# Attention before a routed expert layer: the global queries' scores and maxima go ahead of an even iteration's values, and GpSimd's half of the weight split behind the scalings

## Chip, cores and metric

The kernel runs on one core of a Trainium2 chip. The time is device microseconds of one execution of the whole program, from its first to its last instruction and what lies around them; the figure for a kernel is the median of its runs. Profiles come from one execution of their own.

## What is computed

Local and global attention feeds a mixture of experts with eight experts. Cut to what matters:

```python
# B, H, Sl, Sg, D = 8, 8, 512, 32, 64; window 32
k_all, v_all = concat([k_g, k_l]), concat([v_g, v_l])
out_g = softmax(scale * q_g @ k_all.T) @ v_all            # 32 global queries see all keys
s_l   = concat([scale * q_l @ k_g.T,                      # local queries see the global keys
                where(|i - j| <= 32, scale * q_l @ k_l.T, -1e9)])   # and a band of local ones
out_l = softmax(s_l) @ v_all
x     = concat([out_g, out_l])  as rows of 512            # 8 * 544 = 4352 rows
# rows with x @ w_skip > 0 go to the expert with the largest x @ w_gate:
out   = x + gate * (relu(x @ w1[e]) @ w2[e])              # other rows keep x
```

All of it is float32.

## The kernel before, in words

**Stages.** The first stage does the attention of all batches and, a few iterations behind, writes the rows, computes the logits of gate and skip, and sorts the rows into lists per expert. The second stage runs the experts one after the other. The change lies in the first stage, in a loop whose order is written out by hand for PE, DVE, ACT and POOL (`manual_schedule`, L700); each of these engines takes its instructions in exactly the order of the code. SP, which issues most DMAs, is ordered by the framework.

**Iterations.** One unit of work `u` is a pair of heads of one batch: 8 batches x 4 pairs = 32 units. Iteration `u` of the loop (L720) works on three units at once: `cur` (scores and exponentials), `prev` = u - 1 (normalization and transposes) and `old` = u - 2 (values). For a unit:

- `scores(hf)` (L336), called for hf = 0 and 1: eight matmuls write the scores of four query blocks into two PSUM banks (`pss`, L343). DVE then reads each bank twice, adding the mask and taking the row minimum of the negated scores (L355); ACT takes the exponential with its sum (L360).
- `normal` and `scale` (L383, L388): DVE sums and inverts (L385, L386); POOL multiplies half of the probabilities (L390). `normal(0)`, `scale(0)` run in the unit's own iteration, `normal(1)`, `scale(1)` at the beginning of the next.
- `turn(hf)` (L424): PE transposes four probability blocks into `pst` (L430), which DVE (hf = 0) or ACT (hf = 1) copies to `ptT` (L433). `turn_g` is DVE's own transpose of the part of the global keys (L458).
- `values`, `values_g` (L462, L487): PE multiplies with the values into two banks `pv` (L474, L481, L493); ACT copies the local queries' part out (L501); `gather_g` (L503): DVE sums the global queries' part (L508, L506).

**Global queries.** For every second unit (u even) the 32 global queries of two head pairs are scored together. `window_g` (L367) writes the scores of the global keys, 64 columns, into free columns of a bank of the *second* score block (columns 320 to 383 of `banks[1]`, L350), ahead of DVE's four reads of this block; `window_min` (L374) takes their minimum behind these reads. In u = 0 they have a bank of their own (`pwg`, L399). At the end of the even iteration, behind the transposes, `scores_g` (L395) issues: four matmul instructions against the 512 local keys into a third bank (`psg`, L405), DVE's minimum over them that carries on the window's (L409), and ACT's exponential over all 640 columns (L414). In the next, odd iteration `normal_g` (L418) inverts the sum and lets POOL scale (L422), behind `scale(1)`; at its end `turn_pg` (L438) transposes the result (L442, L443) for the values of this pair of units, and DVE and ACT copy it (L448, L451).

**PSUM.** Score blocks, `psg` and `psgT` share three banks with the tag `s`; rows, transposes and `psgL` share three with the tag `t`; the values have two (`v`).

**Expert weights.** From u = 4 to u = 19 each iteration ends by splitting half of a weight piece of 128 x 1024 in two parts (`split`, L175, called at L803): ACT casts it to the high part (L181) and POOL subtracts this to get the low part (L182). POOL's subtraction so stands in its queue ahead of the next iteration's `scale(1)`, the global scaling and `scale(0)`. The pieces are loaded by SP into two buffers (L159); a load into a buffer waits for the subtraction that read it last.

**Order of one iteration before**, as far as it matters: `scores(0)`; `normal(1)`, `scale(1)` of prev, and for odd u `normal_g`; the rows of an earlier batch; `values` and `values_g` of old; `turn_g(0)`; `normal(0)`, `scale(0)`, `scores(1)`; `gather_g`; `turn_g(1)`; `turn(0)`, `turn(1)` of prev; for odd u `turn_pg`; for even u `scores_g`; up to two of the sends of list entries on POOL; the weight load and split.

Of the kernel before, what the change touches and what calls it, by code (L numbers as in the profile page):

```python
# [10 lines left out]
F32 = mybir.dt.float32  # L11
# [17 lines left out]
QB = 64  # L29
# [14 lines left out]
def kernel(  # L44
# [25 lines left out]
    def ps_v(name):  # L70
        return ps.tile([P, 512], F32, tag="v", name=name, bufs=2)
# [70 lines left out]
    class Weights:  # L142
# [29 lines left out]
                        ),  # L172
                    )

        def split(self, eng, parts=1):  # L175
            if self.done < parts * self.n:
                i, k = divmod(self.done, parts)
                self.done += 1
                sl = slice(k * WC // parts, (k + 1) * WC // parts)
                hi, lo, raw = self.view(i, "h")[:, sl], self.view(i, "l")[:, sl], self.raw[i][:, sl]  # L180
                nc.scalar.copy(hi, raw)  # L181
                eng.tensor_sub(lo, raw, hi.bitcast(F32))  # L182

    weights = {0: Weights(0, wpool)}

    with ExitStack() as actx:
        stage = actx.enter_context(tc.tile_pool(name="stage", bufs=2))
# [132 lines left out]
        def pair(u):  # L320
# [12 lines left out]
            pg = pgs[u // 2]  # L333
            pgTs = {}

            def scores(hf):  # L336

                banks = [ps_s("pss") for _ in range(2)]
                for j in range(2):
                    for odd in range(2):  # L340
                        w = 4 * hf + 2 * j + odd
                        for h in range(2):
                            nc.tensor.matmul(  # L343
                                banks[odd][head(h ^ odd), j * W:(j + 1) * W],
                                q[head(h), w * QB:(w + 1) * QB], window(k[head(h)], w),
                                start=True, stop=True, skip_group_check=True,
                            )
                last = hf == 1 and u % 2 == 0 and u > 0
                if last:
                    window_g(banks[1][:, 2 * W:2 * W + QB])  # L350
                for odd in range(2):
                    for j in range(2):
                        i = 4 * hf + 2 * j + odd
                        m = m_first if i == 0 else m_last if i == NB - 1 else (m_even, m_odd)[odd]
                        nc.vector.tensor_tensor_reduce(  # L355
                            out=pt[:, i, :], in0=banks[odd][:, j * W:(j + 1) * W], in1=m,
                            scale=-0.125, scalar=3.0e38, op0=ALU.add, op1=ALU.min,
                            accum_out=nmx[:, i:i + 1],
                        )
                        nc.scalar.activation(  # L360
                            pt[:, i, :], pt[:, i, :], AF.Exp, bias=nmx[:, i:i + 1],
                            scale=-1.0, accum_out=sums[:, i, 0:1],
                        )
                if last:
                    window_min(banks[1][:, 2 * W:2 * W + QB])

            def window_g(dst):  # L367
                for w in range(2):
# [25 lines left out]

            def scores_g():  # L395

                sumg = sumgt[u // 2 % 2]
                if u == 0:
                    pwg = ps_v("pwg")  # L399
                    window_g(pwg[:, 0:QB])  # L400
                    window_min(pwg[:, 0:QB])
                psg = ps_s("psg")
                for w in range(2):
                    k4 = ks[(u + w) % NQ].rearrange("d r (f g) m -> d g r f m", f=2)
                    nc.tensor.matmul(  # L405
                        psg[w * QB:(w + 1) * QB, :], qgs[b % 2][:, p + w, :],
                        k4[:, 0:4, 0:4], start=True, stop=True,
                    )
                nc.vector.tensor_tensor_reduce(  # L409
                    out=sg[:, 0:512], in0=psg[:, 0:512], in1=m_glob,  # L410
                    scale=-0.125, scalar=nmg[:, 0:1], op0=ALU.add, op1=ALU.min,
                    accum_out=nmg[:, 1:2],
                )
                nc.scalar.activation(  # L414
                    pg, sg, AF.Exp, bias=nmg[:, 1:2], scale=-1.0, accum_out=sumg[:, 0:1],
                )

            def normal_g():  # L418
# [84 lines left out]
            def gather_g(odd):  # L503
# [7 lines left out]
                    )  # L511

            return SimpleNamespace(
                scores=scores, normal=normal, scale=scale, scores_g=scores_g,
                normal_g=normal_g, turn=turn, turn_pg=turn_pg, turn_g=turn_g,
                values=values, values_g=values_g, gather_g=gather_g,
            )
# [182 lines left out]
        with tc.manual_schedule(engines=engines):  # L700
            nc.vector.memset(ones, 1.0)
            load_pair(0)
            warm = ps_t("warm")
            for i in range(WARM):
                nc.tensor.matmul(
                    warm, ones, ones.unsqueeze(1).to_broadcast([P, 4, P]), start=True, stop=True
                )
            consts_early()
            for t in sumt + sumgt:
                nc.vector.memset(t, 1.0e-9)  # L710
            clear_batch(0)
            load_qg(0)
            load_pair(1)
            consts_masks()
            load_v(0)
            load_vg(0)
            load_v(1)
            make_identity(nc, ident)
            prev, old, first = None, None, slice(0, 1)
            for u in range(NU + 2):  # L720
                if u < NU and u % NP == 2 and u // NP + 1 < B:
                    load_qg(u // NP + 1)
                    load_vg(u // NP + 1)
                if u + 2 < NU:
                    load_pair(u + 2)
                if 2 <= u + 1 < NU:
                    load_v(u + 1)
                cur = pair(u) if u < NU else None

                def seam():  # L730
                    tick(1 if u < NU - 4 else 2)
                    if u >= NU - 2:
                        send_some(1)

                def late_rows():
                    for b, k in LATE_ROWS.get(u, ()):
                        batch_rows(b, k)
                    if u == NU - 1:
                        for k in range(5):
                            batch_rows(B - 1, k, (0,))  # L740

                if cur:
                    cur.scores(0)
                if u == 0:
                    consts_pool()
                if prev:
                    prev.normal(1)
                    prev.scale(1)
                    if u % 2 == 1:
                        prev.normal_g()  # L750
                bp, kp = divmod(u - 6, NP)
                if 0 <= bp < B - 3:
                    batch_rows(bp, kp)
                    if kp == 3 and bp % 4 == 3:
                        batch_rows(bp, 4)
                seam()
                if old:
                    old.values(0)
                    old.values(1)
                    old.values_g()  # L760
                if prev:
                    prev.turn_g(0)
                seam()
                if cur:
                    cur.normal(0)
                    cur.scale(0)
                    cur.scores(1)
                seam()
                if old:
                    old.gather_g(0)  # L770
                    old.gather_g(1)
                if prev:
                    prev.turn_g(1)
                late_rows()
                seam()
                if prev:
                    prev.turn(0)
                    prev.turn(1)
                seam()
                if u == NU:  # L780
                    index(first, 0)
                    gather(xfirst, six[:, 0, 0, :], (B - 1) * S)
                if prev and u % 2 == 1:
                    prev.turn_pg()
                if cur and u % 2 == 0:
                    cur.scores_g()
                seam()
                if u == 1:
                    clear_batch(1)
                    consts_late()  # L790
                send_some(2 if u < NU - 3 else 4)
                seam()
                prev, old = cur, prev
                if u == NU - 1:
                    tick(len(stages))
                    send_some(len(sends))
                    slots(first, 0)
                if u == 3:
                    weights[0].load()
                if u >= 4:  # L800
                    if u % 2 == 0:
                        weights[0].load()
                    weights[0].split(nc.gpsimd, 2)  # L803
            for k in range(5):
                batch_rows(B - 1, k, (1,))

# [277 lines left out]
```

## Time and profile before

| | |
|---|---|
| median of 3 runs | 502.52 us (501.07 to 505.88) |
| the profiled execution | 501.2 us |
| its span, first to last instruction | 499.4 us |
| busy PE / PEld / DVE / ACT / POOL | 454.5 / 367.2 / 300.0 / 290.8 / 228.2 us |
| granted TensorE clock, mean | 0.987 |
| HBM read and written | 82.91 and 14.67 MB |

Instructions are named by engine, line and the tiles they write and read: `PE pss L343` is a matmul of line 343 into `pss`. PE is the tensor engine, PEld its weight load (which overlaps it), DVE the vector engine, ACT the scalar engine, POOL GpSimd, SP the queue that issues DMAs. Views used:

- busy time by stretch: for each stretch of time (us from the span's start) the busy time of each engine with its instructions, the granted clock, the DMA engines' busy share and GB/s;
- waits: who waited for whom, total us, times, longest;
- timeline: start, duration, engine, line, operation, out<-in, shape; equal neighbours are merged (x16), and then the duration is that of all of them. In brackets: how long the engine had been idle before, and what ended that. Matmuls are pipelined: the next may start before the printed end, so the time that one costs PE is read from start to start.

Every fp32 matmul shows as two instructions on PE.

### The profile page before, as it was taken

The numbers are of one execution on the slowest core, as the hardware profiler recorded it, in microseconds if no ns is written. First come the engines' busy times: TensorE is split into PE (matmuls) and PEld (weight loads), VectorE is DVE, ScalarE is ACT, GpSimd is POOL, SyncE is SP. The second block draws the span as 40 slices with busy tenths as digits, with TensorE's granted clock in tenths as the row PEclk, the third lists the DMA queues.
The fourth block names the chain that finished last, engine by engine and source line by source line (L and its number), as shares of the span: only waits on it lengthen the run. The fifth ranks groups of instructions, "written<-read, shape, count | busy, mean of one in ns | idle before, by whom it ended". The sixth has DMA issues, their size and how long they took to land. (4 is left out here: it accounts for less than half of the span.)

```text
span 499.4 us, 13645 instructions
## 1 busy us (share of the span) xinstructions
PE 454.5 (91%) x4962; PEld 367.2 (74%) x4962; DVE 300.0 (60%) x1221; ACT 290.8 (58%) x883; POOL 228.2 (46%) x236
## 2 busy tenths in 40 slices
PE   8898999999989998888699999999999999999991
PEld 3575676676666776566597979798978989788881
DVE  6886767877657867784344318783923848157210
ACT  5688999899877888765342208481713635245200
POOL 6556666668864667767345015142300431023200
PEclk9999999999999999999799999999999999999997
DMA  8989888888977798720446406975740849203100
GB/s 250 274 294 319 255 278 243 286 281 188 282 207 229 241 190 265 162 65 2 150 170 170 158 24 197 366 235 191 249 153 7 278 174 323 82 26 129 46 15 17
DMA packets 50545, 93.32 MB, mean 187 GB/s; under 512 B 15596, under 2 KB 19948, under 8 KB 50448
## 3 DMA queue, kind: packets, MB, share of 16 engines
q1 hardware_dynamic: 44624, 81.83, 52.5%
q0 software_dynamic: 5824, 10.25, 6.2%
q8 instruction: 55, 0.90, 0.8%
q14 instruction: 42, 0.34, 0.2%
HBM read 82.91 MB, written 14.67 MB: 195 GB/s over the span
## 5 line engine op out<-in xcount | busy, mean ns | idle before, releaser
L360 ACT ACTIVATE prob<-prob,nmx 128x160 f32<-128x160 f32 x256 | 106.4, 418 | 16.4 <-DVE nmx L355 14.9
L390 POOL TENSOR_TENSOR prob<-prob,inv 128x640 f32<-128x640 f32 x64 | 80.1, 1257 | 32.1 <-ACT prob L360 15.4
L853 ACT ACTIVATE hh<-ph 128x256 fp32r<-128x256 f32 x72 | 27.7, 384 | 79.5 <-PE ph L848 74.1
L930 POOL DMA_INDIRECT out_dram<-yo,six x12 | 12.2, 1018 | 130.0 <-DVE yo L929 112.1
L864 PE MATMUL py<-w2h,hh 128*128 128x512 f32 x144 | 57.1, 397 | 0.0
L864 PE MATMUL py<-w2h,hlw 128*128 128x512 f32 x144 | 56.8, 395 | 0.0
L864 PE MATMUL py<-w2l,hh 128*128 128x512 f32 x144 | 56.7, 394 | 0.0
L343 PE MATMUL pss<-ks,qs 64*64 64x160 f32 x1024 | 50.9, 303 | 2.5 <-DVE nmx L355 1.6
L848 PE MATMUL ph<-xh,w1h 128*128 128x256 f32 x288 | 46.6, 284 | 3.7 <-ACT xh L834 1.5
L474 PEld LDWEIGHTS pv<-ptT,vw 128*64 128x64 f32 x1024 | 39.6, 137 | 12.1 <-issue 4.6
L360 ACT ACTIVATION_READ_ACCUMULATOR prob<-prob,nmx 128x1 f32 x256 | 48.3, 189 | 0.0
L343 PEld LDWEIGHTS pss<-ks,qs 64*64 64x64 f32 x1024 | 33.6, 132 | 19.7 <-issue 13.5
L854 DVE SCALAR_TENSOR_TENSOR hlw<-ph,hh 128x256 fp32r<-128x256 f32 x72 | 30.2, 420 | 29.4 <-ACT hh L853 24.1
L474 PE MATMUL pv<-ptT,vw 128*64 128x64 f32 (+1 forms) x1024 | 44.4, 237 | 2.9 <-issue 1.3
L848 PE MATMUL ph<-xh,w1l 128*128 128x256 f32 x288 | 45.5, 280 | 0.0
L848 PE MATMUL ph<-xl,w1h 128*128 128x256 f32 x288 | 45.4, 280 | 0.0
L848 PEld LDWEIGHTS ph<-xh,w1h 128*128 128x128 f32 x288 | 39.5, 192 | 6.6 <-issue 4.3
L430 PE MATMUL pst<-ident,prob 128*128 128x128 f32 x256 | 37.8, 282 | 6.2 <-POOL prob L390 5.0
L631 POOL DMA_INDIRECT lst<-dat,slu x34 | 34.3, 1008 | 19.1 <-DVE cni L949 10.6
L848 PEld LDWEIGHTS ph<-xh,w1l 128*128 128x128 f32 x288 | 39.2, 191 | 0.0
L848 PEld LDWEIGHTS ph<-xl,w1h 128*128 128x128 f32 x288 | 38.9, 190 | 0.0
L182 DVE TENSOR_TENSOR w1l<-raw,w1h 128x1024 fp32r<-128x1024 f32 x28 | 34.1, 1219 | 6.6 <-ACT w1h L181 5.0
(178 smaller groups left out, 939.7 us busy)
## 6 DMA issues: line engine op xcount, KB each, us to landing
raw<-in_w_dram SPq DMA_DIRECT2D x60, 512.0 KB
vw<-in_v_dram SPq DMA_DIRECT2D x32, 512.0 KB
ks<-in_kT_dram SPq DMA_DIRECT2D x32, 400.0 KB
out_dram<-xr SPq DMA_DIRECT2D x32, 256.0 KB
qs<-in_qT_dram SPq DMA_DIRECT2D x31, 256.0 KB
vgs<-in_vgl_dram SPq DMA_DIRECT2D x32, 64.0 KB
raw<-in_w_dram POOLq DMA_DIRECT2D x4, 512.0 KB
lst<-dat,slu POOLq DMA_INDIRECT x34
```

The lines of the kernel that those rows point to most:

```text
L182: eng.tensor_sub(lo, raw, hi.bitcast(F32))
L343: nc.tensor.matmul(banks[odd][head(h ^ odd), j * W:(j + 1) * W], q[head(h), w * QB:(w + 1) * QB], window(k[head(h)], w), start=True, stop= ...
L360: nc.scalar.activation(pt[:, i, :], pt[:, i, :], AF.Exp, bias=nmx[:, i:i + 1], scale=-1.0, accum_out=sums[:, i, 0:1],)
L390: nc.gpsimd.tensor_mul(pt[:, sl, :], pt[:, sl, :], inv[:, sl].unsqueeze(2).to_broadcast([P, 4, W]),)
L430: nc.tensor.transpose(pst[:, i * P:(i + 1) * P], pt[:, 4 * hf + i, 0:KW], ident)
L474: nc.tensor.matmul(pv[head(h), j * 96:j * 96 + n], vv[:, w, head(h)], ptT[:, w, h ^ odd, 0:n], start=j == 0, stop=False, skip_group_check= ...
L631: ins = nc.gpsimd.indirect_dma_start(out=lst, out_offset=bass.IndirectOffsetOnAxis(ap=slu[:, t:t + 1], axis=0), in_=dat[:, bs[j], t - 4 * ...
L848: nc.tensor.matmul(ph[:, 0:GRP], hl[a][:, c, f * P:(f + 1) * P], bb[:, c, :], start=i == 0, stop=i == 3 * NC - 1,)
L853: nc.scalar.activation(hh[:, f, :], ph[:, 0:GRP], AF.Relu)
L854: nc.vector.scalar_tensor_tensor(hlw[:, f, :], ph[:, 0:GRP], 0.0, hh[:, f, :].bitcast(F32), ALU.max, ALU.subtract,)
L864: nc.tensor.matmul(py, a[:, f, ts_], hl[bb][:, f, :], start=f == 0 and i == 0, stop=f == NF - 1 and i == 2,)
L930: ins = nc.gpsimd.indirect_dma_start(out=out, out_offset=bass.IndirectOffsetOnAxis(ap=sidx, axis=0), in_=yo, in_offset=None, bounds_check= ...
```

## The change

Three things move, and nothing else:

1. In an even iteration `window_g`, `window_min` and the matmuls and maxima of `scores_g` come between the rows of the earlier batch and the values of `old`. The window part now goes into free columns of `banks[1]` of the *first* score block, after the four DVE reads of that block have been issued; u = 0 is no exception any more.
2. The exponential of the global scores (now `exp_g`) stays where `scores_g` was.
3. `split` gets a list for POOL's subtraction; what is in it is issued in the next iteration behind `scale(0)` and `scores(1)`. ACT's cast stays.

```diff
-        def split(self, eng, parts=1):
+        def split(self, eng, parts=1, later=None):
...
                 nc.scalar.copy(hi, raw)
-                eng.tensor_sub(lo, raw, hi.bitcast(F32))
+
+                def rest():
+                    eng.tensor_sub(lo, raw, hi.bitcast(F32))
+
+                if later is None:
+                    rest()
+                else:
+                    later.append(rest)
...
+    subs = []
...
+            sides = {}
+
             def scores(hf):
...
-                last = hf == 1 and u % 2 == 0 and u > 0
+                last = hf == 0 and u % 2 == 0
                 if last:
-                    window_g(banks[1][:, 2 * W:2 * W + QB])
+                    side = banks[1][:, 2 * W:2 * W + QB]
...
                 if last:
-                    window_min(banks[1][:, 2 * W:2 * W + QB])
+                    sides[0] = side
...
             def scores_g():
-                sumg = sumgt[u // 2 % 2]
-                if u == 0:
-                    pwg = ps_v("pwg")
-                    window_g(pwg[:, 0:QB])
-                    window_min(pwg[:, 0:QB])
+                window_g(sides[0])
+                window_min(sides[0])
                 psg = ps_s("psg")
...
+
+            def exp_g():
                 nc.scalar.activation(
-                    pg, sg, AF.Exp, bias=nmg[:, 1:2], scale=-1.0, accum_out=sumg[:, 0:1],
+                    pg, sg, AF.Exp, bias=nmg[:, 1:2], scale=-1.0,
+                    accum_out=sumgt[u // 2 % 2][:, 0:1],
                 )
...
                 seam()
+                if cur and u % 2 == 0:
+                    cur.scores_g()
                 if old:
                     old.values(0)
                     old.values(1)
...
                     cur.scores(1)
+                while subs:
+                    subs.pop()()
                 seam()
...
                 if cur and u % 2 == 0:
-                    cur.scores_g()
+                    cur.exp_g()
...
-                    weights[0].split(nc.gpsimd, 2)
+                    weights[0].split(nc.gpsimd, 2, subs)
```

More of the change, by code (lines that the diff above doesn't have):

```diff
@@ L513, in pair @@
             return SimpleNamespace(
-                scores=scores, normal=normal, scale=scale, scores_g=scores_g,
+                scores=scores, normal=normal, scale=scale, scores_g=scores_g, exp_g=exp_g,
                 normal_g=normal_g, turn=turn, turn_pg=turn_pg, turn_g=turn_g,
```

## The prediction

> **What bounds the kernel now.** The page shows attention up to about 240 us, then the expert layers, which the change does not touch; they would only move. I read the busy time by stretch first. Iterations come in pairs: u even (with the scores of the global queries) and u odd. The bounds of the rows below are starts of a first score block: u = 4 to 20 (eight pairs), then u = 11 (odd), u = 12 (even), and u = 20 to the end of u = 31.
>
> ```profile
> 28.45:137.35 108.90, 100.11 (x1693) 73.00 (x1692) 81.15 (x480) 97.93 (x366) 75.56 (x69) 1.00 0.90 274
> 75.57:82.54 6.97, 5.81 (x104) 4.51 (x102) 5.10 (x31) 6.36 (x24) 4.45 (x4) 1.00 0.92 276
> 82.54:88.63 6.09, 6.09 (x105) 4.38 (x105) 4.56 (x29) 5.64 (x23) 4.15 (x4) 1.00 0.69 209
> 137.35:228.00 90.65, 81.33 (x1328) 60.37 (x1327) 66.05 (x394) 71.75 (x271) 61.13 (x65) 1.00 0.67 187
> ```
>
> The columns are PE, PEld, DVE, ACT, POOL, clock, DMA share, GB/s. The even iteration is all PE (6.09 of 6.09 us); one in two has a logits matmul more and takes 7.09 (68.48 to 75.57, rows below). The odd one is 6.97 us for 5.81 us of PE: something else sets it. The waits by engine, from 10 to 236 us, say what (total, times, longest):
>
> ```profile
> PE psgT L442 <- POOL probg L422: 5.6, 10, 0.6
> PE pst L430 <- POOL prob L390: 5.0, 10, 1.2
> ```
> ```profile
> ACT probg L414 <- DVE nmg L409: 9.9, 13, 1.7
> ACT xT L501 <- PE pv L493: 7.1, 8, 2.2
> ACT ptT L448 <- DVE ptT L448: 2.4, 10, 0.4
> ```
>
> PE waits for GpSimd's scalings, 10.6 us in all, and ACT waits 9.9 us for the maxima of the global scores. The timeline of u = 10 and 11 shows the chain behind it, PE first, then POOL, then ACT:
>
> ```profile
> 72.62 0.72 PE L343 MATMUL pss<-ks,qs 64*64 64x160 f32 x16
> 73.27 0.34 PE L369 MATMUL pss<-ks,qgs 128*64 128x64 f32 x4
> 73.54 1.09 PE L430 MATMUL pst<-ident,prob 128*128 128x128 f32 x8
> 74.56 1.08 PE L405 MATMUL psg<-ks,qgs 128*64 128x512 f32 x4
> 75.57 0.77 PE L343 MATMUL pss<-ks,qs 64*64 64x160 f32 x16
> 76.27 0.66 PE L540 MATMUL pr<-ident,xT 128*128 128x128 f32 x4
> 76.86 1.35 PE L474 MATMUL pv<-ptT,vw 128*64 128x96 f32 x32
> ...
> 78.22 0.67 PE L493 MATMUL pv<-pgT,vgs 64*64 64x128 f32 x16
> 78.71 0.72 PE L343 MATMUL pss<-ks,qs 64*64 64x160 f32 x16
> 79.37 0.66 PE L430 MATMUL pst<-ident,prob 128*128 128x128 f32 x4
> 80.63 0.66 PE L430 MATMUL pst<-ident,prob 128*128 128x128 f32 x4 [0.60 <-POOL prob L390]
> 81.84 0.66 PE L442 MATMUL psgT<-ident,probg 128*128 128x128 f32 x4 [0.55 <-POOL probg L422]
> ```
> ```profile
> 78.09 1.27 POOL L182 TENSOR_TENSOR w1l<-raw,w1h 128x512 fp32r<-128x512 f32 x1 [4.48 <-ACT w1h L181]
> 79.32 1.25 POOL L390 TENSOR_TENSOR prob<-prob,inv 128x640 f32<-128x640 f32 x1
> 80.53 1.25 POOL L422 TENSOR_TENSOR probg<-probg,ing 128x640 f32<-128x640 f32 x1
> ```
> ```profile
> 75.41 0.56 ACT L433 COPY ptT<-pst 128x512 f32<-128x512 f32 x1
> 76.58 0.83 ACT L414 ACTIVATE probg<-smg,nmg 128x640 f32<-128x640 f32 x1 [0.61 <-DVE nmg L409]
> ```
>
> Global scores on PE (74.56), their maxima on DVE, the global exponential on ACT (76.58), the weight cast behind it, the subtraction on POOL (78.09), the two scalings (79.32, 80.53), PE (81.84): one chain through five engines. It ends 6.97 us after 75.57 whatever PE has to do.
>
> **The change, part by part.** No instruction is added or removed except that u = 0 no longer has a bank of its own for its four window matmuls. *The subtraction goes behind the scalings.* It takes 79.32 - 78.09 = 1.23 us off POOL's part of the chain and waits for no cast any more; its own new place, after the first-half scaling, has room, for POOL is busy 4.45 of 6.97 us. *The exponential stays, its maxima come earlier.* ACT's 0.61 us wait goes. Both together: in the odd iteration the scalings start when the maxima and sums of its own first block are through, and I get 6.1 us for it (work of PE 75.57 to 79.37, 1.02 for eight transposes, 0.70 for the five of the global part: 5.52, with about 0.6 of waits left), 0.85 less.
>
> *The price is at the new place.* The window part (L369) now goes into the second bank of the first score block, after the four DVE reads of that block have been put in the queue; before, it went into the bank ahead of the reads. The waits above show that this program holds two accesses of one PSUM bank apart even if both read, and read different columns: ACT's copy L448 waited for DVE's copy L448 of the same bank 10 times, 2.4 us. So I take it that the window matmuls wait until the last of the four reads has ended, and with them all that PE has behind them: the global scores, the values, the second score block, the transposes. That no row shows: bounds are nothing (a write beside a read of other columns) and the full wait. I take the full wait, as it is nearest to the L448 row.
>
> The Trainium skill, "PSUM — Partial Sum Buffer", section "PSUM bank collisions raise a hardware error", has the rule for this: guard PSUM "by bank × quadrant (by bank is the simple version), not by address", for writes against reads as well. The L448 row agrees for two reads; no run here shows a write behind a read. By the rule the sum is the one below, without it the first rival's.
>
> Where do the reads stand? Rows of DVE, in order of time, from u = 10 and u = 11:
>
> ```profile
> 68.48 0.42 DVE L448 COPY ptT<-psgT 128x256 f32<-128x256 f32 x1 [0.22 <-PE psgT L442]
> 68.82 0.28 DVE L451 COPY ptT<-psgL 128x128 f32<-128x128 f32 x1
> 69.29 0.33 DVE L355 CUSTOM_DVE_ANT_0 prob<-pss,m_first 128x160 f32<-128x160 f32 x1 [0.19 <-PE pss L343]
> ...
> 70.03 0.32 DVE L355 CUSTOM_DVE_ANT_0 prob<-pss,m_odd 128x160 f32<-128x160 f32 x1
> ```
> ```profile
> 75.23 0.65 DVE L433 COPY ptT<-pst 128x512 f32<-128x512 f32 x1
> 75.80 0.73 DVE L409 CUSTOM_DVE_ANT_0 smg<-psg,m_glob,nmg 128x512 f32<-128x512 f32 x1
> ...
> 79.70 0.16 DVE L385 TENSOR_REDUCE inv<-sumt 128x4 f32<-128x8 f32 x1 [1.45 <-ACT prob L360]
> ...
> 81.67 0.65 DVE L433 COPY ptT<-pst 128x512 f32<-128x512 f32 x1
> ```
>
> The fourth read ends at 70.35, 1.87 us after the block began; PE is through with the rows of the batch after 1.29 (75.57 to 76.86), with a logits matmul after 2.29. So even as DVE stands now, 0.6 us are lost in every second even iteration. But DVE will be later, for a ring closes that was open. PE's second score block of the even iteration sends DVE and ACT on; ACT's exponential, cast and four exponentials of the odd iteration hold DVE's sums (79.70 waits 1.45 us for ACT today); behind these stand DVE's reads, copies and then the four reads that PE now waits for. Today PE does not wait for those. The ring, once round for a pair:
>
> - PE second score block (even) to ACT's copy: 75.41 - 72.62 = 2.79, and the copy, 0.5.
> - ACT: global exponential, cast and four exponentials to DVE's sums, 79.70 - 76.58 = 3.12.
> - DVE: sums, four reads, sums of the global rows, transpose, 81.67 - 79.70 = 1.97; copy L433, 75.80 - 75.23 = 0.57.
> - DVE: copies L448 and L451, 0.34 and 0.28; four reads, 70.35 - 69.29 = 1.06.
> - PE: window part 73.54 - 73.27 = 0.27, global scores 75.57 - 74.56 = 1.01, values 78.22 - 76.86 = 1.36, their global part 0.49, and the second block again.
>
> The sum is 13.76, with a handover to PE 13.8 us. A pair takes 108.90 / 8 = 13.61 today (6.09 + 6.97 = 13.06 without the logits, 14.06 with). In the ring the logits matmul (1.0 us) hides in the stall, the rest of it does not: of an even iteration of 13.8 - 6.1 = 7.7 us, 6.09 is work and 1.6 stall. So u = 4 to 19: 8 x 13.8 - 108.90 = **+1.5 us**. Bounds: -6.8 (8 x 0.85, no stall) and +4 (14.1 each, since route steps on DVE come into the ring).
>
> *Outside.* From u = 20 the pairs take 90.65 / 6 = 15.1 us and there is no cast: the ring (13.3) is not full, but the stall itself remains. From u = 26 PE has no rows of earlier batches at this place, so it would be ready 0.70 us after the block began (75.57 to 76.27), and the fourth read is much later, for u = 30:
>
> ```profile
> 213.23 0.77 PE L343 MATMUL pss<-ks,qs 64*64 64x160 f32 x16
> 216.21 0.32 DVE L355 CUSTOM_DVE_ANT_0 prob<-pss,m_odd 128x160 f32<-128x160 f32 x1
> ```
>
> It ends 3.3 us after, so 2.6 us of stall; at least 1.87 - 0.70 = 1.2 in u = 26 and 28, 0.6 in 20 and 24: 6.2 us, less some 2 that PE's waits for POOL give back there: **+4** (0 to +7). At the start, u = 0 now needs the second pair's keys right behind the first score block, and u = 2 has the constants of DVE ahead of the four reads: **+2** (0 to +3), an estimate by the same kind of stall.
>
> *SP.* The weight load waits for the subtraction that frees its buffer, and this comes some 5 us later in the iteration; keys and values are queued behind it on SP. I cost this at nothing, as PE nowhere waits for them in the views above; the third rival is the case that it isn't.
>
> **Sum.** +1.5 + 4 + 2 = +7.5 on the profiled execution's 501.2 us (span 499.4): 508.7. That execution lay 1.3 us under the median of the runs shown, 502.5 (501.07 to 505.88), so I predict **510 us**.
>
> **Rivals.** *First: the window matmuls don't wait for the reads* (other side). Place: L369 at the head of the global scores. For it: the columns are free of each other; against: the L448 row. The even iterations keep 6.09 and 7.09 and the odd ones take 6.1: 8 x 0.85 = 6.8 off, less about 2 where the global scores wait for the bank that ACT's copy L448 still reads, and some 1 off outside: 501.2 - 5.8 + 1.3, about 497. It decides as soon as the wait at L369 is under 0.8 us a pair. Chance 0.15.
>
> *Second: the stall is there, but the ring doesn't fill,* because DVE gets to the four reads as it does now, 1.87 us in. Then an even iteration without logits loses 0.6, one with them nothing, and every odd one gains 0.85: 4 x 0.25 + 4 x 0.85 = 4.4 gained in the middle, some 4 lost outside: 502. For it: DVE today is ready only 0.2 us before PE needs it (the 0.22 and 0.19 in the rows of 68.48 and 69.29), so little tells on which side it falls; against: with the odd iteration shorter, the same DVE and ACT work ends later in it. Chance 0.22.
>
> *Third: the keys come late,* because SP stands at the weight load. One us lost in each of the six even iterations with such a load on top: 516. Against: DMA engines are busy 0.90, not 1. Chance 0.05.
>
> **How the numbers follow.** The forecast has 0.58. Within the bounds of its own terms it runs from 503 to 516. The first rival lies at 497, the second at 502; taking all but half of the first and the top of the third gives 498 to 516. A measurement of this kernel tells about 1%, 5 us, from no change. Faster than 497.5: half of the first rival, 0.08. Slower than 507.5: three quarters and more of the forecast and the third, about 0.57. The rest, 0.35, is within 1%.
>
> **What would show it.** In the changed kernel's timeline the window matmuls (L369) of an even iteration without logits start some 1.5 us after the batch's transposes, released by DVE's read of the scores, and the wait list has PE waiting for this read as its largest wait. ACT's wait for the global maxima is gone, PE's waits for POOL fall from 10.6 us to under 5, odd iterations take about 6.1 and even ones 7.7 us. If L369 starts within 0.2 us of the transposes, the step on the bank is wrong; if it waits but starts about 1.9 us into the iteration, the ring is; if PE waits for a DMA there, the third rival is right.

## The result and the profile after

The changed kernel takes 518.94 us (median of 4 runs, 516.88 to 520.08) beside 504.2 us of the kernel before (4 runs, 501.07 to 508.99): ratio 1.029, 95% interval 1.025 to 1.033, so it is slower. A second series of it gave 519.8 us, 1.030 (1.022 to 1.038). The forecast was 510 us with a range of 498 to 516: the sign was right, the size was not. Line numbers of the changed kernel are higher by about ten: the score matmul L343 is L353, DVE's read of it L355 is L365, the window matmul L369 is L379, the global scores L405 are L412, ACT's copy L433 is L443, the transposes of the rows L540 are L550.

The profiled execution took 516.88 us, its span 515.2 us. Busy time by stretch, with the same starts of score blocks as bounds: u = 4 to 20, u = 11, u = 12, and u = 20 to the start of u = 31 (columns as in the first view of the prediction):

```profile
31.80:142.25 110.45, 97.79 (x1694) 73.47 (x1693) 79.07 (x479) 96.60 (x364) 74.63 (x68) 1.00 0.80 249
79.59:85.65 6.06, 5.65 (x102) 4.54 (x102) 4.30 (x30) 6.06 (x24) 3.84 (x4) 1.00 0.90 289
85.65:92.98 7.33, 6.04 (x106) 4.50 (x105) 5.27 (x30) 5.85 (x24) 4.80 (x5) 1.00 0.75 272
142.25:231.50 89.25, 74.01 (x1232) 55.51 (x1231) 59.91 (x360) 65.95 (x248) 57.80 (x62) 1.00 0.68 196
```

The stretch before the first bound is 31.80 us, 3.35 more than before. The middle is 110.45 us, 1.55 more, with odd iterations of 6.06 us (6.1 forecast) and even ones without logits of 7.33 (7.7 forecast). The end (the kernel before has its u = 31 at 219.99) is longer by 11.51 - 3.35 - 1.55 = 6.6 us. PE's largest waits, from 10 to 236 us:

```profile
PE pss L379 <- DVE nmx L365: 12.2, 9, 3.3
PE pr L550 <- ACT ptT L443: 4.9, 8, 0.9
...
PE psgT L452 <- POOL probg L432: 1.4, 5, 0.6
...
PE pst L440 <- POOL prob L400: 0.7, 1, 0.7
```

The first row is the announced wait: the window matmuls for DVE's reads of the scores. The last two are the waits for POOL, 10.6 us before and 2.1 now; ACT's wait for the global maxima is gone. The second row was not announced: the rows of an earlier batch wait for ACT's copy of the transposes. Both stand in u = 12; DVE, ACT and PE in order of time:

```profile
86.81 0.58 ACT L443 COPY ptT<-pst 128x512 f32<-128x512 f32 x1
...
87.44 0.66 PE L550 MATMUL pr<-ident,xT 128*128 128x128 f32 x4 [0.92 <-ACT ptT L443]
...
88.09 0.32 DVE L365 CUSTOM_DVE_ANT_0 prob<-pss,m_odd 128x160 f32<-128x160 f32 x1
...
88.47 0.34 PE L379 MATMUL pss<-ks,qgs 128*64 128x64 f32 x4 [0.38 <-DVE nmx L365]
```

The fourth read begins at 88.09 and is through at 88.41; the window matmuls start at 88.47, right behind it. So the wait is where it was put, but only 0.38 us of this iteration's stall is at L379, and 0.92 us stands ahead of it at L550. The window matmuls start 0.38 us behind the rows, not the forecast 1.5, and 2.82 us into the iteration; of the other signs set for this place (within 0.2 us, or about 1.9 us into the iteration) neither came out. In the middle's iterations with logits (u = 6, 10, 14 and 18) PE does not wait at L379 at all.

The next table has all profiles that follow, in us; "rest" runs from the start of u = 31 to the end of the span.

| kernel | start of u = 4 | u = 4 to 20 | u = 20 to 31 | rest | median | ratio to before (95%) |
|---|---|---|---|---|---|---|
| before | 28.45 | 108.90 | 82.64 | 279.4 | 503.9 to 504.9 | |
| before, second profile | 28.13 | 108.93 | 82.96 | 280.7 | | |
| changed | 31.80 | 110.45 | 89.25 | 283.7 | 518.94 | 1.029 (1.025 to 1.033) |
| changed, second profile | 32.59 | 110.50 | 87.75 | 289.5 | 519.8 | 1.030 (1.022 to 1.038) |
| order alone | 32.77 | 115.72 | 85.02 | 287.1 | 523.59 | 1.037 (1.030 to 1.044) |
| late subtraction alone | 28.36 | 105.25 | 81.29 | 284.4 | 500.12 | 0.988 (0.982 to 0.994) |
| window ahead of the reads | 27.96 | 106.63 | 83.00 | 284.8 | 505.84 | 1.002 (0.998 to 1.006) |
| window in the first bank | 31.26 | 108.06 | 83.42 | 283.2 | 509.25 | 1.009 (1.005 to 1.012) |
| window in a bank of its own | 28.40 | 107.45 | 83.97 | 285.4 | 505.34 | 1.000 (0.996 to 1.004) |
| new order in u = 4 to 19 only | 29.37 | 109.87 | 81.32 | 282.4 | 506.5 | 1.007 (1.003 to 1.011) |
| changed, cast in the odd iteration | 32.58 | 109.27 | 86.88 | 285.5 | 518.32 | 1.029 (1.019 to 1.039) |
| late subtraction, cast in the odd iteration | 28.11 | 104.17 | 81.20 | 284.6 | 498.59 | 0.989 (0.983 to 0.995) |
| late subtraction, global scores ahead of the transposes | 28.20 | 105.24 | 83.55 | 279.4 | 498.86 | 0.991 (0.986 to 0.995) |
| the same, cast in the odd iteration | 29.25 | 103.11 | 83.06 | 280.0 | 498.1 | 0.985 (0.978 to 0.993) |

### The profile page after: what moved, and what is told of

It is laid out like the page before. It is cut to its first block, busy times and chain, and to the rows that moved or that the text cites. A ratio compares the mean times of both kernels' runs of the same rounds, so it can differ in the third digit from the quotient of the medians.

```text
span 515.2 us, 13635 instructions
## 1 busy us (share of the span) xinstructions
PE 452.2 (88%) x4962; PEld 369.3 (72%) x4962; DVE 297.2 (58%) x1221; ACT 289.5 (56%) x883; POOL 227.9 (44%) x236
## 5 line engine op out<-in xcount | busy, mean ns | idle before, releaser
L944 POOL DMA_INDIRECT out_dram<-yo,six x12 | 12.2, 1018 | 136.3 <-DVE yo L943 118.4
L484 PEld LDWEIGHTS pv<-ptT,vw 128*64 128x64 f32 x1024 | 40.8, 138 | 17.4 <-issue 8.9
L353 PE MATMUL pss<-ks,qs 64*64 64x160 f32 x1024 | 50.5, 303 | 1.3 <-DVE nmx L365 0.7
L484 PE MATMUL pv<-ptT,vw 128*64 128x64 f32 (+1 forms) x1024 | 42.9, 237 | 4.6 <-ACT prob L370 1.6
L353 PEld LDWEIGHTS pss<-ks,qs 64*64 64x64 f32 x1024 | 33.7, 133 | 9.4 <-issue 3.2
L365 DVE CUSTOM_DVE_ANT_0 prob<-pss,m_even 128x160 f32<-128x160 f32 x96 | 28.1, 317 | 18.8 <-PE pss L353 18.7
```

What stands on the lines that cost most here:

```text
L353: nc.tensor.matmul(banks[odd][head(h ^ odd), j * W:(j + 1) * W], q[head(h), w * QB:(w + 1) * QB], window(k[head(h)], w), start=True, stop= ...
L365: nc.vector.tensor_tensor_reduce(out=pt[:, i, :], in0=banks[odd][:, j * W:(j + 1) * W], in1=m, scale=-0.125, scalar=3.0e38, op0=ALU.add, o ...
L484: nc.tensor.matmul(pv[head(h), j * 96:j * 96 + n], vv[:, w, head(h)], ptT[:, w, h ^ odd, 0:n], start=j == 0, stop=False, skip_group_check= ...
L944: ins = nc.gpsimd.indirect_dma_start(out=out, out_offset=bass.IndirectOffsetOnAxis(ap=sidx, axis=0), in_=yo, in_offset=None, bounds_check= ...
```

## The experiments

The theory: a write into a bank waits for every read of that bank, PE stands at the window matmuls for DVE's fourth read, and in the middle this closes a ring through ACT, DVE and PE. Rivals: the late subtraction costs the time (A); PE would wait for DVE there whatever the bank (B, E); the middle carries the loss (C); the pairs are not set by ACT (D).

### The two parts apart

The order alone leaves the subtraction where it was; the late subtraction alone is the kernel before with a list behind the second score block.

```diff
-                    weights[0].split(nc.gpsimd, 2, subs)
+                    weights[0].split(nc.gpsimd, 2)
```

> The order of the global scores alone, with the subtraction left where it was before the change. Theory (PE waits at the window matmuls for DVE's fourth read of the same bank, and a ring of 13.8 us per pair closes): the waits at L379 stay as they are, the odd iterations lose part of their gain because POOL's subtraction of 1.23 us is back in their chain; 519 to 523 us, where the changed kernel has 518.9. Rival A (the late subtraction, and the weight load that waits for it on SP, cost the time): back to 502 to 506.

```diff
                     cur.scores(1)
+                while subs:
+                    subs.pop()()
...
-                    weights[0].split(nc.gpsimd, 2)
+                    weights[0].split(nc.gpsimd, 2, subs)
```

> The late subtraction alone, on the kernel before. Theory: no wait is added, PE's waits for POOL (10.6 us before) fall by up to 1.23 us in each of the odd iterations 5 to 19; 496 to 501 us, where before has 504.2. Rival A (the late subtraction costs the time): 513 or more.

Measured: 523.59 us for the order alone, 500.12 us for the subtraction alone. The first is 0.6 us above the expected: its middle takes 115.72 us, its odd iterations 7.53, more than the 6.97 of before, and PE's waits for POOL are back at 10.1 us. Rival A is out: the late subtraction, with its late weight load on SP, is a gain of 1.2% (0.6 to 1.8%). The first of the next rows is its middle, 3.65 us shorter than before; the others are ACT's wait for the global maxima and PE's waits:

```profile
28.36:133.61 105.25, 98.35 (x1694) 72.94 (x1693) 79.50 (x480) 96.63 (x364) 74.51 (x68) 1.00 0.90 282
```
```profile
ACT probg L422 <- DVE nmg L417: 11.6, 15, 1.7
```
```profile
PE pr L548 <- ACT ptT L441: 4.5, 7, 0.9
PE psgT L450 <- POOL probg L430: 2.6, 5, 0.6
...
PE pst L438 <- POOL prob L398: 1.6, 3, 0.7
```

Two things are to be seen. ACT still waits for the maxima (11.6 us), and yet the odd iterations from u = 5 to 13 are down from 6.97 to 5.60 or 5.80 us: the late subtraction alone does that. The even ones are longer for it, 7.08 us for 6.09 in u = 8 and 7.83 for 7.09 in u = 6, so a pair gains 3.65 / 8 = 0.46 us in the mean. And PE's wait for ACT's copy, 4.5 us (0.4 before), is here without any wait at the window matmuls; that it comes with the shorter odd iteration, as ACT is no faster, is my reading.

### The window part ahead of the reads, in the other bank, and in a bank of its own

```diff
                 if last:
                     side = banks[1][:, 2 * W:2 * W + QB]
+                    window_g(side)
...
-                    sides[0] = side
+                    window_min(side)
...
-                window_g(sides[0])
-                window_min(sides[0])
```

> The changed kernel with the window matmuls in the same bank, but issued ahead of DVE's four reads (and the minimum behind them). Nothing writes the bank behind a read any more. Theory: the wait of PE at the window matmuls is gone in the middle, at u = 2 and from u = 26 on; pairs of about 13.1 us in the middle, 497 to 504 us in all (504 if the 4.3 us that the changed kernel lost inside the seventh expert stay). Rival B (the wait is not the bank's: DVE is late for PE at this place anyhow, and the wait only moves to the next matmul that needs DVE): 513 to 519.

```diff
-                    side = banks[1][:, 2 * W:2 * W + QB]
+                    side = banks[0][:, 2 * W:2 * W + QB]
```

> The changed kernel with the window part in the first of the two banks of the block (DVE reads that bank first, so its last read ends two reads, 0.65 us, sooner). Theory (dependency by bank, not by address): PE waits for the second read, not the fourth; 0.65 us less at u = 2 and in each of the six even iterations from u = 20, and 0.3 to 0.65 less in the eight of the middle, where the ring falls to 13.15 us and PE's own work takes over: 510 to 513 us. Rival B, or a wait on the whole block or on DVE's position: within 2 us of the changed kernel's 518.9.

```diff
...
             def scores_g():
-                window_g(sides[0])
-                window_min(sides[0])
+                pwg = ps_t("pwg")
+                window_g(pwg[:, 0:QB])
+                window_min(pwg[:, 0:QB])
```

> The changed kernel, every instruction in the same order on every engine, but the window part in a PSUM bank of its own from the three of the rows and transposes. Theory (PE waits at L379 for reads of the same bank, and for nothing else of DVE): no wait of PE for DVE's score reads is left at the window matmuls, 504 to 509 us (505.8 was had with the window part ahead of the reads; up to 3 us more where the three banks are short). Rival E (the place in the order costs the time, whatever the bank): 515 or more. If the seventh run of expert matmuls takes 25.8 us or more, as in the four profiles with the window part behind the fourth read, it goes by PE's order of instructions; if 24.0 to 24.4, by something that the waits bring.

Measured: 505.84, 509.25 and 505.34 us, where the changed kernel has 518.94 and 519.8. The second edit changes nothing but the bank, and takes 9.7 us off. Here is u = 30 of the changed kernel and then of this one, the last reads and the window matmuls:

```profile
224.84 0.32 DVE L365 CUSTOM_DVE_ANT_0 prob<-pss,m_odd 128x160 f32<-128x160 f32 x1
225.09 0.08 DVE L365 DVE_READ_ACCUMULATOR2_ANT nmx<- 128x1 f32 x1
```
```profile
225.22 0.34 PE L379 MATMUL pss<-ks,qgs 128*64 128x64 f32 x4 [2.69 <-DVE nmx L365]
```
```profile
217.66 0.32 DVE L365 CUSTOM_DVE_ANT_0 prob<-pss,m_even 128x160 f32<-128x160 f32 x1
217.91 0.08 DVE L365 DVE_READ_ACCUMULATOR2_ANT nmx<- 128x1 f32 x1
217.91 0.32 DVE L365 CUSTOM_DVE_ANT_0 prob<-pss,m_odd 128x160 f32<-128x160 f32 x1
218.15 0.08 DVE L365 DVE_READ_ACCUMULATOR2_ANT nmx<- 128x1 f32 x1
218.15 0.32 DVE L365 CUSTOM_DVE_ANT_0 prob<-pss,m_odd 128x160 f32<-128x160 f32 x1
```
```profile
218.04 0.34 PE L379 MATMUL pss<-ks,qgs 128*64 128x64 f32 x4 [0.93 <-DVE nmx L365]
```

With the window part in the second bank PE starts 0.05 us after the fourth read; with it in the first bank it starts 0.05 us after the second read (217.91 + 0.08), while the third and fourth are still to end. The columns are free of each other in both. So the program holds PE by the bank. The trace agrees here with the rule of the Trainium skill that the prediction named ("PSUM — Partial Sum Buffer", section "PSUM bank collisions raise a hardware error"), to guard by bank and not by address. With a bank of its own, nothing of DVE's reads of the scores is left in PE's waits at the window matmuls, though every engine has the same order; these are PE's largest waits there, and its wait for the logits' transposes:

```profile
PE pr L544 <- ACT ptT L437: 4.8, 7, 0.9
PE pr L527 <- ACT xr L545: 1.8, 1, 1.8
...
PE pq L563 <- ACT ptT L437: 1.5, 4, 0.4
```

Rivals B and E are out. The theory's own number was too good for the first edit, though: 505.84 us, not 497 to 504. Its middle is 106.63 us, 13.3 per pair and not 13.1; the odd iterations from u = 5 to 13 keep 6.06 to 6.4 us where the late subtraction alone has 5.6 to 5.8. So without the wait the early order is still 5 us behind the late subtraction alone.

### Where along the attention the loss is

```diff
+            early = 4 <= u < 20
...
-                if cur and u % 2 == 0:
+                if cur and u % 2 == 0 and 4 <= u < 20:
                     cur.scores_g()
...
                 if cur and u % 2 == 0:
+                    if not 4 <= u < 20:
+                        cur.scores_g()
                     cur.exp_g()
```

Outside these units the window part is in the second score block, as before.

> The changed kernel with the new order only in u = 4 to 19; u = 0, 2 and from 20 on are as before (window part in the second block, global scores behind the transposes), the late subtraction stays. Theory (13.8 us per pair in the middle as in the changed kernel, and the larger part of the loss at u = 2 and from u = 20 on, by the wait at L379 outside the ring): the start of u = 4 back to 28.4 us, the middle 110 to 111, u = 20 to 30 back to 81 to 83, in all 505 to 508 us. Rival C (the middle carries the loss and the ends only show it later): 513 or more.

Measured: 506.5 us, and by stretch:

```profile
29.37:139.24 109.87, 97.50 (x1694) 73.37 (x1693) 78.47 (x477) 96.01 (x360) 74.61 (x68) 1.00 0.83 261
139.24:220.56 81.32, 73.47 (x1232) 55.02 (x1231) 59.83 (x363) 66.65 (x253) 55.17 (x60) 1.00 0.79 219
```

Of the 14.7 us, 12.4 go with the new order at both ends, so rival C is out. The start of u = 4 is 1 us later than expected, the middle 0.1 us under the expected 110. In u = 2 the changed kernel shows the price; PE, then DVE:

```profile
15.65 0.85 PE L353 MATMUL pss<-ks,qs 64*64 64x160 f32 x16
19.84 0.48 PE L379 MATMUL pss<-ks,qgs 128*64 128x64 f32 x4 [3.33 <-DVE nmx L365]
20.11 1.92 PE L412 MATMUL psg<-ks,qgs 128*64 128x512 f32 x4
21.82 1.73 PE L484 MATMUL pv<-ptT,vw 128*64 128x96 f32 x32
```
```profile
16.94 0.27 DVE L284 MEMSET qgs<- 128x256 f32 x1
...
18.58 0.28 DVE L276 MEMSET pads<- 128x272 f32 x1
18.78 0.26 DVE L365 CUSTOM_DVE_ANT_0 prob<-pss,m_first 128x160 f32<-128x160 f32 x1
...
19.46 0.32 DVE L365 CUSTOM_DVE_ANT_0 prob<-pss,m_odd 128x160 f32<-128x160 f32 x1
```

DVE has 1.84 us of constants (16.94 to 18.78) ahead of the four reads, and PE stands 3.33 us. Behind the stall the global scores take 1.92 us where they take 1.03 in u = 12: the granted clock is 0.83 over u = 2 and 1.00 over u = 12. The last section takes up such a drop.

### Is it ACT that sets the pairs?

```diff
                     if u % 2 == 0:
                         weights[0].load()
-                    weights[0].split(nc.gpsimd, 2, subs)
+                    else:
+                        for _ in range(2):
+                            weights[0].split(nc.gpsimd, 2, subs)
```

> The changed kernel with both halves of a weight piece cast in the odd iteration, none in the even one: the cast leaves the place between the global exponential and the odd iteration's four exponentials, where the ring has it (about 0.5 us), and goes where ACT has slack (it waits 1.28 us for the values there). Theory (a ring through ACT sets the pairs): u = 4 to 20 falls from 110.45 to 106 to 108 us, 514 to 517 in all. Rival D (the pairs are set by PE's waits for a bank and not by what ACT does ahead of them): the middle stays at 110 to 111.

The time is 518.32 us, ratio 1.029 (1.019 to 1.039): above the 514 to 517 expected. The middle is 109.27 us, also outside. But the five pairs u = 6 to 15, first of the changed kernel and then of this one, are 0.45 us shorter each, as 0.5 us less in the ring wants it:

```profile
44.66:113.78 69.12, 62.24 (x1074) 46.73 (x1073) 49.68 (x301) 61.49 (x232) 44.98 (x42) 1.00 0.77 253
```
```profile
45.45:112.32 66.87, 61.82 (x1075) 46.57 (x1074) 49.22 (x299) 61.72 (x229) 45.45 (x43) 1.00 0.81 259
```

From u = 16 to 19 a net 1.1 of the 2.25 us are lost again, with u = 17 at 7.78 us, before the edit 6.54; POOL has both halves of the subtraction ahead of two sends, and the scalings behind them:

```profile
119.10 2.50 POOL L184 TENSOR_TENSOR w2l<-raw,w2h 128x512 fp32r<-128x512 f32 x2
121.80 1.20 POOL L641 DMA_INDIRECT lst<-dat,slu  x1 [0.19 <-issue]
123.30 0.98 POOL L641 DMA_INDIRECT lst<-dat,slu  x1 [0.30 <-DVE pgT L468]
124.29 1.28 POOL L400 TENSOR_TENSOR prob<-prob,inv 128x640 f32<-128x640 f32 x1
```

So ACT is in the ring (rival D is out for these pairs). It holds PE at the rows more than at the window matmuls: PE's waits for ACT's copy at L550 fall from 4.9 to 2.6 us, those at L379 stay, 11.8 us for 12.2. The edit as a whole shows no gain.

### Versions without the wait

Three kernels start from the late subtraction alone. One has the cast in the odd iterations as above; one has the global scores and maxima ahead of the transposes, and the exponential where it was; one has both.

> The late subtraction alone on the kernel before (500.1 us), with the cast moved in the same way, both halves in the odd iteration. If the kernel with the late subtraction is held by the same ACT chain (its pairs of 13.4 and 12.9 us hold a wait of PE for ACT's copy L441 of 0.66 to 0.91 us): 495 to 498 us. If that wait has another cause: 499 to 502.

```diff
+                if cur and u % 2 == 0:
+                    cur.scores_g()
                 if prev:
                     prev.turn(0)
                     prev.turn(1)
...
                 if cur and u % 2 == 0:
-                    cur.scores_g()
+                    cur.exp_g()
```

> The kernel before with the late subtraction, and the matmuls and maxima of the global scores ahead of the transposes (behind the second score block, whose bank the window part shares ahead of the reads, as before); the exponential stays. Theory (what was left for the early order to gain is ACT's wait of 11.6 us for the global maxima, and this place has no write behind a read): the wait goes, 496 to 499 us beside 500.1 of the late subtraction alone. If that wait is covered: 499 to 502.

> The same with both halves of a weight piece cast in the odd iteration: 494 to 498 us if both gains add up, 498 to 500 if the second is covered by the first.

Measured: 498.59 us (ratio 0.989, 0.983 to 0.995), 498.86 us (0.991, 0.986 to 0.995) and 498.1 us (0.985, 0.978 to 0.993). All beat the kernel before, by 0.9 to 1.5%; none can be told from the late subtraction alone (0.988), so whether the two gains add up is not shown. The second one does what it should with ACT's wait:

```profile
ACT probg L423 <- DVE nmg L416: 0.7, 2, 0.5
```

Its middle takes 105.24 us beside 105.25. Two parts of it differ, though; u = 4 to 13 and u = 14 to 19, first of the late subtraction alone, then of this version:

```profile
28.36:92.53 64.17, 60.04 (x1043) 44.93 (x1042) 47.69 (x293) 59.06 (x223) 40.95 (x34) 1.00 0.91 299
92.53:133.61 41.08, 38.31 (x653) 28.00 (x652) 31.82 (x188) 37.56 (x143) 33.57 (x35) 1.00 0.90 255
```
```profile
28.20:90.40 62.20, 59.73 (x1043) 44.76 (x1042) 47.93 (x292) 59.71 (x223) 40.82 (x34) 1.00 0.91 303
90.40:133.44 43.04, 39.32 (x652) 28.44 (x651) 32.76 (x188) 38.49 (x143) 33.72 (x35) 1.00 0.91 255
```

The first ten iterations are 2.0 us shorter and the last six 2.0 us longer. In these six PE stops three times, for 0.43, 0.39 and 0.53 us, and the profile names nothing that it waits for. With the cast moved as well, the middle is 103.11 us beside 104.17. So by these rows ACT's 11.6 us of waiting were worth 2.0 us in the first ten iterations and nothing in the sum; the greater part was idle time off the path. The time fell in the range expected, but that the wait is the reason is not shown.

### A second profile of each kernel

> The changed kernel once more, for a second profile: whether the 9.75 us of u = 30 (2.69 us of waiting at L379, with 1.10 us of an idle DVE ahead of the reads that nothing in the profile explains) and the 2.09 us gap of PE inside the seventh expert recur. If they belong to the change, both do; if they are of one execution, u = 30 takes 7 to 8 us and the seventh expert 36.4 us, and the time is still 517 to 520.

> The kernel before once more, for a second profile: from the start of u = 31 to the end of the span it took 279.4 us in the first one, and 282.4 to 289.5 in all others so far. If the first profile was an execution with a short expert stage, this one shows 282 to 286 and the attention again 220 us up to u = 31.

The middle repeats within 0.1 us in both kernels. The 9.75 us of u = 30 do not repeat (6.89 in the second profile), and its stall at L379 is 1.42 us there, not 2.69. The stop of PE in the seventh run of expert matmuls does repeat in the changed kernel:

```profile
426.08 0.28 PE L862 MATMUL ph<-xh,w1h 128*128 128x256 f32 x1 [2.45 <-issue]
```

That run takes 28.5 and 28.9 us in the changed kernel, 25.8 and 26.0 with the order alone and with the cast moved, 26.3 with a bank of its own, 24.1 and 25.4 in the two profiles of the kernel before, 24.0 to 24.9 elsewhere. By the mark set ahead, the 26.3 us would put it down to PE's order of instructions; but the kernel with the window part in the first bank has this order too, and takes 24.9. So neither PE's order nor the stalls in the attention mark it off. One thing can be read from the traces: eight stops of PE among the expert matmuls are longer than 0.6 us and named "issue", and in each PE goes on 2.3 to 2.6 us after a transfer of 16 KB on the queue that the profile calls "instruction" has begun (at 423.62 for the row above). So PE probably stood there for instructions; why they came late is not shown. The "rest" of the kernel before was short in both profiles (279.4 and 280.7 us), not 282 to 286 as expected.

## Why the prediction was right or wrong

**The subtraction.** Right in sign, wrong in the working. The odd iterations lost 1.2 to 1.4 us by it alone, not 0.85 by this and the maxima together, but the even ones grew by 0.7 to 1.0 where they were to keep their time: a pair gained 0.46 us in the mean. The maxima were worth little: ACT's wait for them was taken to be on the chain because the row names DVE as the releaser, and without the wait the first ten iterations gain 2.0 us and the whole middle nothing.

**The price at the new place.** Right: a write waits for the reads of its bank, and the two edits of the bank show it. Without the wait the time is 505.3 us.

**The ring.** The size came out, 110.45 / 8 = 13.81 us per pair for 13.8 and +1.55 us in the middle for +1.5, but in part by luck. The ring had PE wait at DVE's reads in every pair. In the pairs with logits it does not, and u = 6 and 7 take 13.69 us, u = 10 and 11 take 13.61, with a bank of its own 13.68 and 13.61: this wait does not set them. Where it does, in u = 8 and 9 and in u = 12 and 13, pairs of 13.70 and 13.72 us fall to 13.26 and 13.27. In the middle the larger part of the stall is at the rows, which wait for ACT's copy (4.3 us, beside 3.4 at the window matmuls), and that part is there without the bank's wait too (3.8 us with a bank of its own). The ring had PE's handover at DVE's reads alone; ACT's copy closes it as well, at the rows, which stand ahead of the window matmuls.

**Outside.** This is the step that failed: the start was put too low, and the expert layers, which "would only move", were put at nothing.

- *The start*, +2 and at most +3, measured +3.35 us and, by the second profiles, +4.5. One estimate of 2 us stood for a stall that measured 3.33 us and a dropped clock behind it: u = 2 took 10.08 us for 4.54, and u = 0 and 1 gave back 2.7. With the window part ahead of the reads, or in a bank of its own, u = 4 starts at 27.96 and 28.40 us, no later than before.
- *The end*, +4, measured +6.6 and, by the second profiles, 87.75 - 82.96 = +4.8. Of the first, 3.0 us stand in u = 30 alone (9.75 for 6.75), which did not repeat; of the second, 1.6 in the dropped clock of the last section. Without these, 3.6 and 3.2 are left, so the size was about right. The stalls at the window matmuls add up to 7.0 and 5.0 us there, for 6.2 estimated. Not all of the loss is the wait for the bank: u = 23, 25 and 27 took 7.36, 9.46 and 7.81 us where they had 6.96, 8.79 and 7.08, and with a bank of its own they take 7.35, 9.49 and 7.70.
- *The expert layers*, here the stretch from u = 31 to the end, took 4.3 us longer in the first profiles and 8.8 in the second.

Of the 9 us between the forecast and 518.94, the start has 1.4 in the first profile, the end 2.6 and the expert layers 4.3; the rest is the basis.

**The basis.** The median of 3 runs, 502.5 us, was low: 503.9 to 504.9 in the four series since. The sum was put 1.3 us above the profiled execution; about 3 would have been right. And the terms' own bounds do not give 503 as the lower end: -6.8, 0 and 0 lead to 495.7.

**What stays open.** Up to u = 31 the changed kernel loses 11.5 us (10.8 by the second profiles), in all 14.7 to 15.9. The other 3 to 5 us stand from u = 31 on, nearly all of which the change does not touch, and this stretch spreads over 279.4 to 289.5 us in the fourteen profiles. In the first profiles the seventh run of expert matmuls alone is 4.4 us longer (28.5 for 24.1); in the second it is 3.5 longer, and the first run 3.6 (32.8 for 29.1). PE is busy for 257.4 and 259.1 us in this stretch, beside 256.1 and 255.5 before, and the granted clock over it is 0.97 and 0.96, beside 0.98 and 0.98: the greater part of the difference is PE standing still. That it follows from the change isn't shown, and neither is that it doesn't.

**The rivals.** The first, no wait at L369, was priced at 497 us. The kernel that has no wait there takes 505: the early order brings nothing of its own, and in the middle it is 2.2 us behind the late subtraction alone (107.45 for 105.25). Why is open. One reading is that it takes cover away: before, the global matmuls (1.0 us) stood between the transposes and the next block, and DVE and ACT copied the transposes meanwhile; moved, PE comes to the logits' transposes in the odd iteration and waits up to 0.4 us for ACT's copy (the last row of the kernel with a bank of its own), a wait that the late subtraction alone does not have. Against it: with the global scores ahead of the transposes the cover is gone as well, and there this wait does not appear and the first ten iterations are 2.0 us shorter. The second rival (502) failed: the window matmuls of u = 12 start 2.82 us into the iteration, not 1.9. The third failed with the late subtraction alone, which has the same late loads and is faster.

## What to carry to other kernels

Before an instruction is moved ahead, look at what its destination shares: a write into free columns of a PSUM bank waited here for every read of that bank, and a bank of its own took 13.6 us off the changed kernel. An engine's wait in the profile is a gain only if the engine is late for somebody: taking ACT's 11.6 us away bought 2.0 us in ten iterations and nothing over the middle. The cheapest test is to take the wait away by itself, and to compare stretch by stretch, as a gain in one can hide behind a loss in the next. Where one change holds two moves, run each alone: one was worth -1.2% here and the other +3.7%.

## What was not expected of the hardware

The same short stop of PE costs nothing more in one execution and 1.6 us in the next. In u = 21 of the changed kernel PE waits for a copy of ACT; first profile, then second:

```profile
153.70 0.74 PE L533 MATMUL pr<-idw,xTg 128*128 128x137 f32 x4 [1.81 <-ACT xr L551]
154.37 1.34 PE L484 MATMUL pv<-ptT,vw 128*64 128x96 f32 x32
```
```profile
155.50 0.74 PE L533 MATMUL pr<-idw,xTg 128*128 128x137 f32 x4 [1.81 <-ACT xr L551]
156.17 1.71 PE L484 MATMUL pv<-ptT,vw 128*64 128x96 f32 x32
```
```profile
149.08:158.44 9.36, 7.23 (x114) 6.00 (x113) 5.27 (x35) 6.95 (x27) 4.91 (x5) 1.00 0.57 190
```
```profile
150.84:161.77 10.93, 8.75 (x114) 7.25 (x113) 5.36 (x36) 7.09 (x28) 4.94 (x6) 0.84 0.59 180
```

The stop is 1.81 us in both. In the first the granted clock stays at 1.00 and the iteration takes 9.36 us; in the second it is 0.84 over 10.93 us (if the low part is at half speed, 0.32 x 10.93 = 3.5 us of it), the values take 1.71 us for 1.34, and the iteration is 1.57 us longer. In the seven profiles with the early order at this place, u = 21 takes 9.36 to 9.41 us in three and 10.93 to 10.98 in four. The Trainium skill, "TensorE: Matmul & The Clock Gate", section "Part 1: The HAM clock gate", has the clock halved after at least one idle window of about 3.4 us, with windows that run on freely. The length agrees with the 3.5 us, and free windows would explain why one of two equal stops was hit; that a whole window must be idle does not agree with a stop of 1.81 us.
